# The first attention's last transposes ahead of the second pair's values, and part of the last tile's stores over three queues

## The chip, the cores and the metric

The kernel runs on one core of one Trainium2 chip. The metric is the device time of one launch in microseconds (us), as the median over several executions; a profile of one execution stands beside it.

## The reference

Sliding-window attention is followed by a feed-forward network. Batch 8, 8 heads, 576 positions, 64 elements per head; each query sees the keys at most 32 positions away. The feed-forward part takes 4608 tokens of 512 values through a hidden layer of 2048 with the tanh form of GELU. Everything is given and taken in float32.

```python
scores = (1 / sqrt(64)) * matmul(q, k.transpose(0, 1, 3, 2))      # q, k, v: (8, 8, 576, 64)
scores = where(abs(i - j) <= 32, scores, -1e9)
attn = softmax(scores)                                            # over the keys
x = matmul(attn, v).transpose(0, 2, 1, 3).reshape(4608, 512)
h = x @ w_in                                                      # 512 x 2048
g = 0.5 * h * (1 + tanh(c * (h + 0.044715 * h**3)))               # c = sqrt(2 / pi)
out = g @ w_out                                                   # 2048 x 512
```

## The kernel before

**Staging.** The attention works by batch `b` and by groups `g`: groups 0 to 3 are the four pairs of heads, group 4 is the tail of the positions. Its result goes, transposed, into a ring `xT`, from which the feed-forward part takes nine tiles `t` of 512 tokens. Batch `b = t + 1` is computed while tile `t` is in its second product (`ffn_out`), after a table (`PLAN`) that names at which matmul which piece is emitted. There is no scheduler behind this: each engine executes its instructions in the order in which the program writes them, and waits only where data or a buffer is missing.

**The start.** Batch 0 has no tile to lie beside. All of its inputs, the weights and the inputs of batch 1 come over SP's queue, one DMA after the other, in the written order: q and k by pairs (`qk`), v by heads (`vs`), then the float32 weights in four blocks (`load_w_in`: the first in two halves, which bring rows 0 to 1 and 2 to 3 of the block's four), batch 1's q and k, and w_out. GpSimd (POOL) casts most of it to float16: q and k by pairs (`cast_early`, L253), v by pairs (`cast_v`, L263), the first two weight blocks (`cast_w`, L190).

For a group the chain is: TensorE transposes q and k (`turn`, L282 and L284) into the PSUM bank `x0`; VectorE (DVE) copies them out (`trans_out`, L289 and L290); TensorE makes the scores (`score`, L354); ScalarE (ACT) takes the exponential (L360); VectorE multiplies with a mask (`mask`, L369); TensorE sums values and weights (`weighed`, L387; it needs the cast v of its pair); ScalarE inverts the sums as exp(-ln) (L401, L402); VectorE multiplies (`spread`, L411) into `xT`. `spin` issues matmuls of 512 columns on zeros that nothing reads.

After that come the first columns of the first product, `ffn_in(0, fc, d0, d1)` (L446): `d0` to `d1` is the part of the 512 rows of w_in taken, and pair `d` of `xT` is what it is multiplied with. Columns 0 to 3 take block 0 of w_in, columns 4 to 7 block 1.

**The end.** The last tile (t = 8) is combined from seven products of half the size (`ffn_out`, n counts them, and `ffn_last`). Its results leave as they become final: two quarter-tiles after n = 2 (on SP), two after n = 4, two after n = 5, two in `ffn_last`. A quarter-tile of 128 tokens is stored in two to five pieces, because batches and positions cut it; of n = 4 and n = 5 there are seven pieces each. Earlier tiles are stored by GpSimd's queue.

**Waits of the DMAs.** In the built program the DMAs of SP and ACT carry one of eight counters in turn, in one common sequence, and each waits, before it is issued, until the DMA that had the same counter eight places before has landed. GpSimd's DMAs have eight counters of their own.

Of the kernel before, what the change touches and what calls it, by code (L numbers as in the profile page):

```python
# [29 lines left out]
def cut(b):  # L30
    return 120 if b else 128


def width(pieces):
    return sum(4 * (p1 - p0) for (_, _, p0, p1) in pieces)
# [26 lines left out]
def kernel(  # L62
# [9 lines left out]
    nc = tc.nc  # L72
# [5 lines left out]
    NT = NTOK // 512  # L78
# [98 lines left out]
    def stage_w():  # L177
        return stage.tile([128, 4, 512], FP32, name="wst", tag="stage")

    def load_w_in(i, w, c0=0, c1=4):  # L180
        nc.sync.dma_start(w[:, c0:c1, :], w_in_v[:, c0:c1, 512 * i:512 * i + 512])  # L181
        return w
# [5 lines left out]
    def cast_w(w, dst, on_dve=2, cs=range(4)):  # L188
        for c in cs:
            (nc.vector if c < on_dve else nc.gpsimd).tensor_copy(dst[:, c, :], w[:, c, :])  # L190

    qk, tails, vs, vtail = load_early(0)
# [6 lines left out]
    qk(6)  # L199
    vs(2, 3)  # L200
    vs(4, 5)
    wi = [load_w_in(0, stage_w(), 0, 2)]
    vs(6, 7)
    load_w_in(0, wi[0], 2, 4)
    wi[1:] = [load_w_in(i, stage_w()) for i in range(1, 4)]

# [4 lines left out]
    def spin(n, width, score=False):  # L211
        ps = psS.tile([128, 2, 512], FP32, name="spin2", tag="S0")[:, 0, :] if score else \
            psO.tile([128, 512], FP32, name="spin", tag="O")
        for _ in range(n):
            nc.tensor.matmul(ps[:, 0:width], idle[:, 0:128], idle[:, 0:width], start=True, stop=True)
# [12 lines left out]
    for i in (0, 3, 4, 1, 2):  # L228
        m, off = masks[i], 0
# [30 lines left out]
    def cast_v(b, pr):  # L260
        vr = raws[b][3]
        hs = slice(2 * pr, 2 * pr + 2)
        nc.gpsimd.tensor_copy(Vs[b % 2][:, 0:4, hs, :], vr[:, :, hs, :])  # L263
# [24 lines left out]
    def trans_out(b, pr, pt):  # L288
        nc.vector.tensor_copy(QTs[b][:, pr, :, 0:128], pt[:, 0:4, :])  # L289
        nc.vector.tensor_copy(  # L290
            KTs[b % 2][:, pr, 0:512].rearrange("d (p j) -> d p j", j=4),
            pt[:, 4:8, :].rearrange("d j p -> d p j"))
# [37 lines left out]
    def halves_of(b, g):  # L330

        if g < 4:
            return [(masks[0], [g], MAIN[0]),
                    (masks[1], [g], MAIN[1]) if b else (masks[3], [g], MAIN_0[1])]
        return [(masks[2], range(NPAIR), TAIL) if b else (masks[4], range(NPAIR), TAIL_0)]
# [9 lines left out]
    def score(b, g):  # L345
        pes = []
        for hf, (m, prs, pieces) in enumerate(halves_of(b, g)):
            w = width(pieces) * len(prs)
            ps = psS.tile([128, 2, 512], FP32, name="ps_s", tag=f"S{hf}")
            for (pr, k0, c, p0, p1, off) in placed(prs, pieces):  # L350
                n = p1 - p0
                for h in range(2):
                    r0 = 64 * h
                    nc.tensor.matmul(  # L354
                        ps[:, h, off:off + 4 * n].rearrange("k (j p) -> k j p", j=4),
                        KTs[b % 2][r0:r0 + 64, pr, k0:k0 + 128],
                        QTs[b][r0:r0 + 64, pr, :, p0:p1], start=True, stop=True)
            pe = ap_.tile([128, 2, w], FP16, name="pe", tag=f"pe{hf}") if g < 4 else \
                tailp.tile([128, 2, w], FP16, name="pet")
            nc.scalar.activation(pe, ps[:, :, 0:w], AF.Exp, scale=SCALE)  # L360
            pes.append(pe)
        groups[(b, g)] = pes
# [42 lines left out]
    def spread(b, g, o, lt):  # L405
        n = size(b, g)
        if g < 4:
            pos, done = b * S % RING, 0
            while done < n:
                e = min(n - done, RING - pos)  # L410
                nc.vector.tensor_tensor(xT[:, g, pos:pos + e], o[:, done:done + e],  # L411
                                        lt[:, done:done + e], op=ALU.mult)
                done, pos = done + e, (pos + e) % RING
        else:
            pos = (b * S + 4 * cut(b)) % RING
            assert pos + n // NPAIR <= RING
            nc.vector.tensor_tensor(
                xT[:, :, pos:pos + n // NPAIR], o[:, 0:n].rearrange("d (r q) -> d r q", r=NPAIR),
                lt[:, 0:n].rearrange("d (r q) -> d r q", r=NPAIR), op=ALU.mult)
# [72 lines left out]
    out_v = out.rearrange("(b p j) f -> b j p f", b=B, j=4)  # L492
    pys = {}

    turn_about = [nc.sync, nc.scalar]

    def store(t, t4, yo, cols=slice(0, 512), eng=None):
        m = 0
        while m < 128:
            b, c = divmod(t * 512 + t4 * 128 + m, S)  # L500
            q0, n = (0, cut(b)) if c < 4 * cut(b) else (cut(b), 144 - cut(b))
            j, p = divmod(c - 4 * q0, n)
            e = min(n - p, 128 - m)
            if t == NT - 1 and eng is None:
                turn_about.reverse()
            (eng or turn_about[0] if t == NT - 1 else eng or nc.gpsimd).dma_start(  # L506
                out_v[b, j, q0 + p:q0 + p + e, cols], yo[m:m + e, cols])
            m += e

    later = []  # L510
# [14 lines left out]
    def ffn_out(t, i):  # L525

        n, blk, f = i // 16, i // 8 % 2, i % 8
        if t == 1 and i > 2 and i in wino["todo"]:
            combine(i)
        a, w, new = WINO[n]  # L530
        end = t == NT - 1
        if i % 16 == 0 and new:
            pys[n % 2] = bank((first(t) + n) % 2)
            if end and n == 4:
                pys["apart"] = psO.tile([128, 512], FP32, name="py2", tag="O")
        py = pys[n % 2].rearrange("p (b c) -> p b c", b=2)
        apart = end and blk and n in (4, 6)
        if a[0] == "A":
            r0, c0 = 8 * (int(a[2]) - 1) + f, 256 * (int(a[1]) - 1) + 128 * blk
            lhsT = gTs[t][:, r0, c0:c0 + 128]  # L540
        else:
            lhsT = wino[a][:, f, 128 * blk:128 * blk + 128]
        one = end and n in (4, 6)
        nc.tensor.matmul(pys["apart"][:, 0:256] if apart else py[:, blk, :], lhsT,  # L544
                         wino[w][:, f, :], start=(new and i % (8 if one else 16) == 0),
                         stop=(i % (8 if one else 16) == (7 if one else 15)),
                         skip_group_check=True)
        if i % 16 < 15:
            return
        yo, left, right = wino["yo"], slice(0, 256), slice(256, 512)  # L550
        C11, C12, C21, C22 = (yo[:, r:r + 2, c] for r in (0, 2) for c in (left, right))

        M1, U2, U3 = C21, C12, C22
        if n == 0:
            nc.vector.tensor_copy(M1, py)
        elif n == 1:
            nc.vector.tensor_tensor(U2, py, M1, op=ALU.add)
        elif n == 2:
            nc.vector.tensor_copy(C11, py)
            if end:  # L560
                for x in range(2):
                    store(t, x, yo[:, x, :], left, nc.sync)
        elif n == 3:
            nc.vector.tensor_tensor(U3, py, M1, op=ALU.add)
        elif n == 4:
            if not end:
                nc.vector.tensor_tensor(C22, py, U3, op=ALU.add)
            else:
                for x, part in enumerate((py[:, 0, :], pys["apart"][:, 0:256])):
                    nc.vector.tensor_tensor(C22[:, x, :], part, U3[:, x, :], op=ALU.add)  # L570
                    store(t, 2 + x, yo[:, 2 + x, :], right)
        elif n == 5:
            nc.vector.tensor_tensor(C21, py, M1, op=ALU.add)  # L573
            for x in range(2):
                store(t, 2 + x, yo[:, 2 + x, :], left if end else slice(0, 512))
# [23 lines left out]
    cast_early(0, 3, both)  # L599
    cast_v(0, 1)  # L600
    cast_v(0, 2)
    cast_w(wi[0], w_in16[:, :, 0:512], 0, (0, 1))
    cast_v(0, 3)
    cast_w(wi[0], w_in16[:, :, 0:512], 0, (2, 3))


    qk, tails, vs, vtail = load_early(1)
# [4 lines left out]
    def turn(g):  # L612
        pt = bank16(0)
        trans_pair(0, g, pt, now=False)
        return pt
# [8 lines left out]
    pt = turn(1)  # L624
# [7 lines left out]
    pt = turn(2)  # L632
# [2 lines left out]
    mask(0, 1, (1,))  # L635
    weighed(0)
    score(0, 2)
    spread(0, 0, *ods[0])
    spin(5, 512)
    weighed(1)  # L640
    pt = turn(3)
    trans_out(0, 3, pt)
    mask(0, 2)
    spin(3, 512, score=True)
    score(0, 3)
    spread(0, 1, *ods[1])
    weighed(2)
# [34 lines left out]
    for fc in range(6, NF):  # L682
        if fc in TURN_0:
# [3 lines left out]
            if pr < 2:  # L687
                pt = psS.tile([128, 2, 8, 128], FP16, name="pt", tag=f"S{pr}")
# [8 lines left out]
    for t in range(NT):  # L697
        b = t + 1
# [18 lines left out]
        for i in range(113 if t else 65):  # L717
            for act in plan.get(i, "").split():
# [11 lines left out]
                elif kind == "t":  # L730
                    pt = psS.tile([128, 2, 8, 128], FP16, name="pt", tag="S1")
# [19 lines left out]
            if t == 0 and i in (38, 40, 55):  # L751
                t4, yo = later.pop(0)
# [41 lines left out]
```

The softmax here doesn't subtract the row's maximum and nothing guards it: scores larger than these inputs give would overflow.

## Time and profile before

| | us |
|---|---|
| median of 4 executions | 311.67 (310.79 to 313.68) |
| the profiled execution's own time | 311.07 |
| its span, first to last instruction | 309.3 |
| TensorE busy | 297.9 (96%) |
| ACT / DVE / POOL busy | 199.9 / 198.4 / 102.2 |
| mean granted TensorE clock | 0.999 |

Busy time of TensorE is modelled for the ends of the matmuls, which are pipelined; a matmul of 512 columns has 379 ns in the rows, while eight in a row take 1.73 us. "PEld" are its weight loads, "SPq", "ACTq" and "POOLq" the queues that issue DMAs. The moved bytes are 50.64 MB, of which 37.50 MB go over SP's queue.

### The profile page before, as it was taken

How to read it: one execution, taken by the hardware profiler on the slowest of the kernel's cores; microseconds unless marked ns; L12 is line 12 of the kernel's file. 1: busy time of each engine (PE TensorE's matmuls, PEld its weight loads, DVE VectorE, ACT ScalarE, POOL GpSimd, SP SyncE). 2: the span in 40 equal slices, each digit the busy share in tenths (PEclk: the TensorE clock that was granted, in tenths of full speed). 3: DMA queues.
4: the chain of work that ended last, by engine and by line, in shares of the span. 5: the costliest groups of instructions: out<-in, count | busy, mean ns of one | idle time of the engine just before them, and what ended most of it. 6: DMA issues, size and time to landing. Idle time of an engine off the chain costs nothing.

```text
span 309.3 us, 6731 instructions
## 1 busy us (share of the span) xinstructions
PE 297.9 (96%) x2643; PEld 187.1 (60%) x2643; DVE 198.4 (64%) x453; ACT 199.9 (65%) x315; POOL 102.2 (33%) x158
## 2 busy tenths in 40 slices
PE   6889999999999999999999999999999999999993
PEld 2553545445784588448854785478647864784583
DVE  5764587867968476947784678666866643632451
ACT  1776477477677776778676876677768676706600
POOL 2647455192029110921093108510710061006000
PEclk9999999999999999999999999999999999999999
DMA  7999999999998998899769965999391022004013
GB/s 200 255 343 370 374 343 199 311 162 149 176 220 192 158 215 119 149 161 230 144 171 155 254 105 140 155 217 172 92 168 34 2 71 67 2 0 136 2 37 100
DMA packets 120061, 50.64 MB, mean 164 GB/s; under 512 B 101327, under 2 KB 113359, under 8 KB 120030
## 3 DMA queue, kind: packets, MB, share of 16 engines
q1 hardware_dynamic: 84329, 37.50, 58.7%
q0 software_dynamic: 34768, 11.54, 30.7%
q10 hardware_dynamic: 933, 1.18, 1.2%
q8 instruction: 20, 0.33, 0.5%
q14 instruction: 11, 0.09, 0.1%
HBM read 37.62 MB, written 9.44 MB: 152 GB/s over the span
## 4 chain that ended last, share of the span: by engine, by line
PE 72%; SPq 12%; DMA 11%; DVE 3%; issue 1%; POOL 0%; DVEq 0%
PE mm L544 30%; PE mm L446 20%; PE ph L446 12%; SPq L139 5%; PE ps_o L387 4%; DMA wst<-in_moe_w_in_dram 3%; PE ps_s L354 3%; DMA qr<-in_q_dram 3%; PE ps_d L387 3%; DMA KT<-k 3%; DMA kr<-in_k_dram 2%; SPq L162 2%; SPq L130 2%; SPq L185 1%; SPq L181 1%
## 5 line engine op out<-in xcount | busy, mean ns | idle before, releaser
L446 PEld LDWEIGHTS <-w_in 128*128 128x128 f16 x576 | 56.0, 98 | 66.5 <-POOL w_in L190 1.3
L446 PE MATMUL mm<-xT,w_in 128*128 128x512 f16 x352 | 86.3, 379 | 0.5 <-DVE xT L411 0.5
L506 POOL DMA_DIRECT2D out_dram<-y x77 | 45.2, 594 | 115.5 <-DVE y L573 114.7
L454 ACT ACTIVATE gT<-mm 128x512 f16<-128x512 f32 x88 | 52.4, 599 | 37.1 <-PE mm L446 37.1
L446 PE MATMUL ph<-xT,w_in 128*128 128x512 f16 x224 | 58.7, 379 | 0.3 <-POOL w_in L190 0.3
L490 DVE TENSOR_TENSOR s<-gT 128x512 f16<-128x512 f16 x64 | 26.9, 420 | 42.1 <-ACT gT L454 42.1
L544 PEld LDWEIGHTS <-s 128*128 128x128 f16 x512 | 48.6, 98 | 7.5
L360 ACT ACTIVATE pe<-ps_s 128x704 f16<-128x704 f32 x64 | 43.3, 727 | 9.2 <-PE ps_s L354 9.2
L544 PE MATMUL mm<-t,s 128*128 128x256 f16 x376 | 45.7, 273 | 0.0
L401 ACT ACTIVATE lt<-ps_d 128x480 f32<-128x480 f32 (+3 forms) x40 | 22.2, 556 | 30.8 <-PE ps_d L387 30.8
L454 ACT ACTIVATE gT<-ph 128x512 f16<-128x512 f32 x56 | 33.0, 600 | 13.0 <-PE ph L446 12.9
L544 PEld LDWEIGHTS <-gT 128*128 128x128 f16 x384 | 36.0, 98 | 7.3
L544 PE MATMUL mm<-w_out,gT 128*128 128x256 f16 x256 | 32.8, 273 | 0.0
L369 DVE TENSOR_TENSOR pe<-pe,mask 128x704 f16<-128x704 f16 x64 | 31.2, 523 | 1.7 <-ACT pe L360 1.6
L411 DVE TENSOR_TENSOR xT<-ps_o,lt 128x480 f16<-128x480 f32 (+5 forms) x38 | 20.2, 549 | 12.5 <-ACT lt L402 12.5
L387 PEld LDWEIGHTS <-V 128*64 128x64 f16 x336 | 18.1, 109 | 10.7 <-issue 5.0
L402 ACT ACTIVATE lt<-lt 128x480 f32<-128x480 f32 (+3 forms) x40 | 23.5, 587 | 1.3
L387 PE MATMUL ps_o<-pe,V 128*64 128x160 f16 (+2 forms) x244 | 21.8, 241 | 0.8 <-POOL V L263 0.4
L87 ACT ACT_TABLE_LOAD x17 | 21.8, 1283 | 1.1 <-PEq L778 0.8
L387 PE MATMUL ps_d<-pe,ones 128*64 128x192 f16 (+2 forms) x264 | 22.4, 235 | 0.0
L170 POOL DMA_DIRECT2D V<-in_v_dram x24 | 22.0, 941 | 0.0
L354 PE MATMUL ps_s<-QT,KT 64*128 64x192 f16 (+5 forms) x336 | 17.9, 227 | 1.1 <-DVE KT L290 1.0
(77 smaller groups left out, 295.9 us busy)
## 6 DMA issues: line engine op xcount, KB each, us to landing
kr<-in_k_dram SPq DMA_DIRECT2D x32, 256.0 KB, 6.8
qr<-in_q_dram SPq DMA_DIRECT2D x6, 1024.0 KB, 7.7
V<-in_v_dram POOLq DMA_DIRECT2D x30, 128.0 KB, 7.9
wst<-in_moe_w_in_dram SPq DMA_DIRECT2D x3, 1024.0 KB, 8.3
wst<-in_moe_w_out_dram SPq DMA_DIRECT2D x3, 1024.0 KB
qr<-in_q_dram SPq DMA_DIRECT2D x8, 256.0 KB
vr<-in_v_dram SPq DMA_DIRECT2D x16, 128.0 KB, 7.5
out_dram<-y POOLq DMA_DIRECT2D x24, 48.0 KB, 2.3
```

Of the source, the lines that this page charges most:

```text
L170: nc.gpsimd.dma_start(V[:, c, :, :], v[b, :, 128 * c:128 * c + 128, :].rearrange("h p d -> p h d"))
L354: nc.tensor.matmul(ps[:, h, off:off + 4 * n].rearrange("k (j p) -> k j p", j=4), KTs[b % 2][r0:r0 + 64, pr, k0:k0 + 128], QTs[b][r0:r0 + 6 ...
L360: nc.scalar.activation(pe, ps[:, :, 0:w], AF.Exp, scale=SCALE)
L369: nc.vector.tensor_tensor(pe, pe, m.rearrange("p (o w) -> p o w", o=1).broadcast_to(list(pe.shape)), op=ALU.mult)
L387: nc.tensor.matmul(bk[r0:r0 + 64, at:at + 4 * n].rearrange("d (j p) -> d j p", j=4)[:, :, p0 - q0:p1 - q0], V[:, c, 2 * pr + h, :] if w == ...
L401: nc.scalar.activation(lt[:, 0:n], d[:, 0:n], AF.Ln)
L402: nc.scalar.activation(lt[:, 0:n], lt[:, 0:n], AF.Exp, scale=-1.0)
L446: nc.tensor.matmul(ph, w_in16[:, dc, fc * 128:fc * 128 + 128], xT[:, dc, t * 512 % RING:t * 512 % RING + 512], start=(dc == 0), stop=(dc = ...
L454: nc.scalar.activation(gTs[t][:, fc, :], phs[fc], AF.Gelu_apprx_tanh)
L490: nc.vector.tensor_tensor(dst, x, y, op=op)
L506: (eng or turn_about[0] if t == NT - 1 else eng or nc.gpsimd).dma_start(out_v[b, j, q0 + p:q0 + p + e, cols], yo[m:m + e, cols])
L544: nc.tensor.matmul(pys["apart"][:, 0:256] if apart else py[:, blk, :], lhsT, wino[w][:, f, :], start=(new and i % (8 if one else 16) == 0) ...
```

## The change

In the start, the v of heads 6 and 7 is loaded ahead of the first half of w_in's first block, where it was between the two halves; GpSimd's casts follow in the same order. In batch 0, `turn(3)` and `trans_out(0, 3)` stand directly after `score(0, 2)`, ahead of the weighing of pair 1; the spins there, five and three, become four in one place. In the end, the stores after n = 4 go round SP, GpSimd and ACT (GpSimd first) where they went round ACT and SP; those after n = 5 go round ACT and SP as before, but begin with ACT where they began with SP.

```diff
     vs(2, 3)
     vs(4, 5)
+    vs(6, 7)
     wi = [load_w_in(0, stage_w(), 0, 2)]
-    vs(6, 7)
     load_w_in(0, wi[0], 2, 4)
...
-    turn_about = [nc.sync, nc.scalar]
+    turn_about, three = [nc.sync, nc.scalar], [nc.sync, nc.gpsimd, nc.scalar]
...
             if t == NT - 1 and eng is None:
-                turn_about.reverse()
-            (eng or turn_about[0] if t == NT - 1 else eng or nc.gpsimd).dma_start(
-                out_v[b, j, q0 + p:q0 + p + e, cols], yo[m:m + e, cols])
+                turn_about.append(turn_about.pop(0))
+            if eng is three:
+                three.append(three.pop(0))
+            q_ = three[0] if eng is three else eng or (turn_about[0] if t == NT - 1 else nc.gpsimd)
+            q_.dma_start(out_v[b, j, q0 + p:q0 + p + e, cols], yo[m:m + e, cols])
...
                     nc.vector.tensor_tensor(C22[:, x, :], part, U3[:, x, :], op=ALU.add)
-                    store(t, 2 + x, yo[:, 2 + x, :], right)
+                    store(t, 2 + x, yo[:, 2 + x, :], right, three)
...
     cast_v(0, 2)
+    cast_v(0, 3)
     cast_w(wi[0], w_in16[:, :, 0:512], 0, (0, 1))
-    cast_v(0, 3)
     cast_w(wi[0], w_in16[:, :, 0:512], 0, (2, 3))
...
     score(0, 2)
+    pt = turn(3)
     spread(0, 0, *ods[0])
-    spin(5, 512)
+    trans_out(0, 3, pt)
+    spin(4, 512)
     weighed(1)
-    pt = turn(3)
-    trans_out(0, 3, pt)
     mask(0, 2)
-    spin(3, 512, score=True)
     score(0, 3)
```

## Prediction

> **What bounds the kernel now.** I read the page's slices first, then the chain of work that ended last, then the timeline around the two places of the change. The chain, in order of time, in three pieces:
>
> ```profile
> 14.61 0.52 SPq L181
> ...
> 15.69 10.50 DMA wst<-in_moe_w_in_dram
> ...
> 26.20 7.93 DMA qr<-in_q_dram
> ...
> 66.90 7.91 DMA KT<-k
> ...
> 74.86 0.46 PE ps_s L354 x8
> ```
>
> Up to 74.8 us the end is set by SP's stream of loads (weights, batch 1, batch 2, the transposes by DMA), not by the attention of batch 0. After that the chain is TensorE's matmuls nearly to the end. The slices agree: DMA is at 9 from the second slice on, at 340 to 374 GB/s while the weights come. Where the attention of batch 0 (12 to 24 us) meets that stream shows in the timeline (start, length, engine, what, idle before and who ended it):
>
> ```profile
> 17.30 1.17 POOL L190 CAST w_in<-wst 128x512 f16<-128x512 f32 x2 [0.87 <-DMA wst<-in_moe_w_in_dram]
> ...
> 19.47 0.61 POOL L263 CAST V<-vr 128x512 f16<-128x512 f32 x1 [1.00 <-DMA vr<-in_v_dram]
> ...
> 20.76 1.20 POOL L190 CAST w_in<-wst 128x512 f16<-128x512 f32 x2 [0.68 <-DMA wst<-in_moe_w_in_dram]
> ...
> 23.52 2.29 POOL L190 CAST w_in<-wst 128x512 f16<-128x512 f32 x4 [1.57 <-DMA wst<-in_moe_w_in_dram]
> ...
> 24.75 0.39 PE L446 MATMUL ph<-xT,w_in 128*128 128x512 f16 x1 [0.17 <-POOL w_in L190]
> ...
> 25.31 1.04 PE L446 MATMUL ph<-xT,w_in 128*128 128x512 f16 x4 [0.17 <-POOL w_in L190]
> ```
>
> To be seen: four loads end GpSimd's idle time one after another, and the last, block 1 of w_in at 23.52, is cast slice by slice while TensorE waits for each slice, the last time at 25.31. Whatever TensorE does before, it passes 25.31 no sooner unless that block lands sooner. Behind it there is next to no slack in the other direction: TensorE is busy 4.69 of the 4.70 us after 25.30, and it reached the scores at 74.86 about when the last transpose landed (busy 4.89 of the 5.00 us from 70). So an early gain is lost, and a delay beyond 25.31 is mostly paid.
>
> **The change part by part: the start.** *Loads.* Same DMAs, same bytes, same counter by place in the sequence; two of 128 KB (v of heads 6 and 7) go past one of 512 KB. What follows, block 0's second half included, keeps its place, so it should land as before: 20.76 and 23.52. Between lie, by the rows above, 19.47 - 17.30 = 2.17 us for the two v, 20.76 - 19.47 = 1.29 us for a half block. Reversed: v at 17.30 - 1.3 or so + 2.17, about 18.0 (was 19.47), and the first half at 19.47 (was 17.30). GpSimd's casts then run: v 18.0 to 18.6, first half 19.47 to 20.7 (two of 0.61), second half from 20.76 as before. GpSimd's queue loses nothing, since the second half is not there earlier.
>
> *Order of the attention.* ACT and DVE keep their sequences; on TensorE eight transposes go past the weighing of pair 1, and 8 spins become 4 (4 x 0.216 us less, with 1.73 us for eight). After `score(0, 2)` (13.62, 0.49 us) the transposes of q can start at once (q's cast ended at 13.55), those of k wait for the cast that ends at 14.51; TensorE is through at about 15.0, was 17.08. Queued behind this 0.4 us wait are four spins and the weighing of pair 1, which needed v's cast, at 15.62, anyway: it goes at 15.9 to 16.7, was 15.67 to 16.5, a loss of 0.2. DVE copies out after `spread(0, 0)` (ends 15.39, unmoved): 15.4 to 16.4, was 17.11 to 18.13. The wait removed is this one:
>
> ```profile
> 18.19 0.49 PE L354 MATMUL ps_s<-QT,KT 64*128 64x160 f16 x10 [0.47 <-DVE KT L290]
> ```
>
> `score(0, 3)` goes at 16.7 (was 18.19), mask 2 at 16.4 to 17.65 (18.05 to 19.31), weighing of pair 2 at 17.25 to 18.1 (18.89 to 19.9). The gain shrinks at once on ACT, which has, in order, ln and exp of pair 1 (0.60 + 0.63), two exponentials of pair 3 (1.46), ln and exp of pair 2 (1.23): from 16.8 they end at 20.7, were 21.2. So `spread(0, 2)` ends at 21.4, was 21.94. What is late next is TensorE's following instruction, `ffn_in(0, 0)`: it needs the first half's casts, at 20.1 and 20.7, ran at 19.84 before; behind it in the queue stands the weighing of pair 3, so at 20.95 to 21.85 (was 20.51 to 21.45), 0.4 later. Then six matmuls to 23.15, four to 24.0, and column 4, whose weights are there at 24.19 as before. `spread(0, 3)` comes at about 23.25 to 23.95 (was 22.86), wanted only after 26. **Sum of the start: 0.0 us.** The cover is the arrival of block 1; it leaves 0.2 us at 24.19 and some 0.6 at 25.31. If block 0 landed half a microsecond later than I say, that would still be hidden. Bounds for the start: a loss of 0.7 (both halves landing together at 20.76: casts to 23.2, column 5 done at 26.8 instead of 26.18); a gain of 0.5, if the denser order let block 1 land that much earlier (nothing in the rows says so).
>
> **TensorE's idle time** [...]. Between the weighing of pair 2 (18.1) and `ffn_in(0, 0)` (20.1) it now stands for about 2.0 us with no spin, where the largest gap of that stretch was about half a microsecond. The trace has one long pause, at the end: the last matmul ends at 304.5, and the granted clock (third value from the end of each row; before it the busy time of TensorE, weight loads, DVE, ACT and POOL, after it DMA share and GB/s) is
>
> ```profile
> 307.50:308.00 0.50, 0.00 (x0) 0.00 (x0) 0.00 (x0) 0.00 (x0) 0.00 (x0) 1.00 0.00 0
> 308.00:308.50 0.50, 0.00 (x0) 0.00 (x0) 0.00 (x0) 0.00 (x0) 0.00 (x0) 0.93 0.00 0
> 308.50:309.30 0.80, 0.00 (x0) 0.00 (x0) 0.00 (x0) 0.00 (x0) 0.00 (x0) 0.50 0.04 10
> ```
>
> so full for some 3.8 us of idling, then half. [...] I take the row: 0.0. If the cover were gone, see the third rival.
>
> **The end.** These are the last DVE result and the last issues, and the waits that SP makes in the store line:
>
> ```profile
> 304.56 0.42 DVE L582 TENSOR_TENSOR y<-py,y 128x256 f32<-128x256 f32 x1 [0.45 <-PE py L544]
> ...
> 305.01 0.80 ACTq L506 DMA_DIRECT2D out_dram<-y  x2
> ...
> 305.59 0.74 SPq L506 DMA_DIRECT2D out_dram<-y  x2
> ...
> L506 SPq EVENT_SEMAPHORE  x4: 17/17/17, 300.0 to 305.5; - x4
> ```
>
> SP's last two stores hold what DVE finished at 304.10, yet go out at 305.59: the first has the counter of an 88 KB store that ACT issued at 303.53, and a wait on SP ends at 305.5. That gives 1.96 us from issue to release. The last issue ends at 306.33, and the span 3.0 us later.
>
> With the change, three of the seven pieces after n = 4 (40, 24 and 24 rows) go to GpSimd, and the counters of all later stores shift. GpSimd: start at 300.65 when DVE is done, 594 ns each by its 77 rows, the second and third after DVE's 301.48, so done by 302.7; 2.3 us to landing (its 48 KB stores; nearest row, for the smaller 16 KB ones it is 2.5): 305.2 at most, two microseconds before the last store lands. Cost 0.0; nobody waits for its counters. After n = 5 ACT issues four pieces from 303.53 (to 305.01, as SP's four did), SP three (to 304.74). Last pieces: SP's 56 rows have a long-landed counter and go at 304.8; SP's 72 rows have that of the 88 rows which SP now issues at 303.53, so 305.5 + 0.09 to 305.95. ACT's 48 rows have that of 40 rows issued at 303.53: 305.5, not 305.01, to 305.87; its 80 rows that of 32 rows issued at 303.87: 303.87 + 1.96 = 305.83, to about 306.27. **Sum: 306.27 against 306.33, -0.05 us**: the wait moves from SP to ACT. Bounds: -0.5 (no counter waited for: ACT's last issue ends at 305.81) and +0.3 (the 40 and 32 rows landing as late as 2.3 us).
>
> [...]
>
> **Total.** 311.07 of the profiled execution - 0.05 = 311.0. The profiled execution is 0.6 below the median of the runs shown, so the same kernel measured anew is 311.67 - 0.05 = **311.6**.
>
> **Rivals.**
> 1. *No change*, as summed: 311.6. Chance 0.72.
> 2. *The end gains its bound*, because landings are quicker than 1.96 us for small pieces: 311.67 - 0.5 = 311.2. For it: two of ACT's four waits hang on pieces of 40 and 32 rows. Against: 80 rows still go last behind another store. 0.10.
> 3. *Slower by the clock.* If the first half of w_in came so late [...], it would work at half clock from there: 12 matmuls (2.6 us) and a weighing (0.9) double, +3.5, of which 0.6 is slack and about 1.2 is taken by later waits of TensorE (0.25 at 31.46, 0.36 at 37.88, 0.19 at 39.73, 0.38 at 46.80). About +1.7: 313.4; without those waits +2.9, 314.6. For it: the spins have gone just there. Against: the same half lands 1.3 us ahead of a load that keeps its place. 0.08.
> 4. *The attention is on the path after all*: the 0.5 us by which `spread(0, 2)` comes earlier, or all of the 1.5 of `score(0, 3)`, reaches the end: 311.2 to 310.2. Against: the wait at 25.31. 0.06.
> The rest, 0.04, is a start that the loads' new order stretches or shortens by a microsecond or more.
>
> **Numbers.** The runs before spread by 2.9 us, so the median itself is good to about 1 us; with the bounds (-1.0 and +1.0 together) and part of rival 3 the range is 309.9 to 313.3. About 1%, 3.1 us, is what a measurement of this kernel can tell from no change: faster 0.02, within 0.93, slower 0.05, the last mostly rival 3.
>
> **What would show it.** Right: GpSimd's w_in casts again from 20.76 and 23.52, L446 waiting for them to 25.3, the L290 wait before `score(0, 3)` gone, a TensorE gap of 2 us before 20.1 at full clock, the KT transposes landing at 74.8, and an ACT wait at 305.8 ahead of the last store. Wrong: block 1 cast before 23.2 or after 23.8, a clock below 1.00 between 18 and 26, a last issue before 305.9 or after 306.6, or GpSimd's stores landing last.

## The result, and the profile after

Median 312.54 us (311.06 to 314.54, 44 executions) against 311.69 us for the kernel before (310.46 to 313.73, 63 executions): a ratio of 1.0027, 95% interval 1.0017 to 1.0038. The change costs **0.85 us** (0.5 to 1.2). That is within 1%, and within the range of the prediction, but it is a loss that many executions resolve, where the forecast was 0.05 us of gain. The profiled execution took 312.19 us, with a span of 310.2.

From the page, the span and the granted clock in 40 slices of 7.8 us:

```profile
span 310.2 us, 6725 instructions
...
PEclk9989999999999999999999999999999999999998
```

The third digit is new: the clock of TensorE falls in the third slice (15.5 to 23.3 us), just where the change thinned its work. The timeline of the start of the changed kernel (start, length, engine, what, idle before and who ended it):

```profile
18.15 0.61 POOL L263 CAST V<-vr 128x512 f16<-128x512 f32 x1 [1.30 <-DMA vr<-in_v_dram]
19.41 2.61 POOL L190 CAST w_in<-wst 128x512 f16<-128x512 f32 x4 [0.65 <-DMA wst<-in_moe_w_in_dram]
...
20.08 0.39 PE L446 MATMUL mm<-xT,w_in 128*128 128x512 f16 x1 [1.69 <-POOL w_in L190]
...
20.96 0.39 PE L446 MATMUL mm<-xT,w_in 128*128 128x512 f16 x1 [0.49 <-POOL w_in L190]
...
23.46 2.29 POOL L190 CAST w_in<-wst 128x512 f16<-128x512 f32 x4 [1.44 <-DMA wst<-in_moe_w_in_dram]
...
27.14 0.59 PE L446 MATMUL mm<-xT,w_in 128*128 128x512 f16 x2
```

In it the casts of v, of the first half and of block 1 of w_in stand where the prediction put them (18.0, 19.47, 23.52), and so do the first two matmuls of `ffn_in(0, 0)` (20.1 and 20.7). But the last row is late. It is the matmul pair that begins the last column of block 1, and in the kernel before it stands here:

```profile
26.18 0.59 PE L446 MATMUL mm<-xT,w_in 128*128 128x512 f16 x2
```

From the first cast of block 1 that is 26.18 - 23.52 = 2.66 us before and 27.14 - 23.46 = 3.68 us after. The table of stretches shows what lies between (us; then busy time and count of TensorE, weight loads, VectorE, ScalarE, GpSimd; then granted clock, DMA share, GB/s). The changed kernel:

```profile
18.00:20.00 2.00, 0.40 (x14) 0.30 (x8) 1.56 (x3) 2.00 (x4) 1.20 (x3) 1.00 1.05 388
20.00:21.40 1.40, 0.82 (x6) 0.31 (x8) 1.08 (x2) 0.69 (x2) 1.40 (x3) 0.99 1.03 395
21.40:24.80 3.40, 3.40 (x26) 1.98 (x25) 0.74 (x2) 2.01 (x3) 1.96 (x5) 0.50 1.05 393
```

The kernel before, same stretches:

```profile
18.00:20.00 2.00, 1.60 (x31) 1.33 (x32) 2.00 (x5) 1.44 (x3) 1.00 (x2) 1.00 1.02 335
20.00:21.40 1.40, 1.34 (x22) 0.88 (x20) 1.07 (x3) 1.19 (x3) 0.72 (x3) 1.00 1.02 392
21.40:24.80 3.40, 2.75 (x19) 1.14 (x13) 1.24 (x2) 2.51 (x3) 1.83 (x4) 1.00 1.05 393
```

TensorE pauses between 18.4 and 21.0, twice (1.69 and 0.49 us); its clock is full all through the pauses and is halved afterwards, from 21.38 to 24.79 by the clock's own records, 3.41 us in which TensorE had work at every moment. Counted from the first cast of block 1, batch 1's first transposes begin 8.55 us later, where the kernel before takes 7.94 us: of the 1.02 us, 0.61 us are left there.

What becomes of them further on, these two profiles do not show. Tile 1 begins its first product at 60.73 (60.12 before) and tile 2 at 93.00 (92.57 before). But two kernels of the experiments below, the end alone and ACT first, have the start of the kernel before and a full clock in it, and their tile 2 begins at 93.00 and 93.09. And the chain of work that ended last in the changed kernel does not pass the late matmuls. At that time it runs through SP's loads:

```profile
15.79 10.32 DMA wst<-in_moe_w_in_dram
...
26.14 7.97 DMA qr<-in_q_dram
```

From the start of tile 2 to that of tile 8 every one of the thirteen profiled executions takes 185.74 us. So what tells them apart lies ahead of tile 2, or behind the last VectorE result.

The second part of the loss is at the end. The last VectorE row and the stores of the last tile, after:

```profile
304.99 0.42 DVE L584 TENSOR_TENSOR y<-py,y 128x256 f32<-128x256 f32 x1 [0.45 <-PE py L546]
...
L509 ACTq DMA_DIRECT2D out_dram<-y x8: 306/348/560, 301.1 to 306.5; - x8
L509 ACTq EVENT_SEMAPHORE  x4: 17/17/17, 292.8 to 305.9; - x4
```

The rows of one line give min, median and max length in ns, then first and last start. Last result to end of the span is 310.2 - 305.41 = 4.79 us; before it was 309.3 - 304.98 = 4.31 us (unrounded spans). I call this the **closing time**. So the 0.9 us between the two spans are 0.43 us from ahead of the end, which is no more than two executions of one kernel can differ by, and 0.48 us of closing time, which repeats from profile to profile (next section).

### The profile page after: what moved, and what is told of

Its sections match the earlier page's. It is cut to its first block, busy times and chain, and to the rows that moved or that the text cites. A ratio compares the mean times of both kernels' runs of the same rounds, so it can differ in the third digit from the quotient of the medians.

```text
span 310.2 us, 6725 instructions
## 1 busy us (share of the span) xinstructions
PE 297.7 (96%) x2639; PEld 187.9 (61%) x2639; DVE 198.9 (64%) x453; ACT 199.7 (64%) x315; POOL 103.7 (33%) x161
## 4 chain that ended last, share of the span: by engine, by line
PE 71%; SPq 11%; DMA 11%; DVE 4%; issue 1%; POOL 0%; DVEq 0%
PE mm L546 30%; PE mm L446 19%; PE ph L446 12%; SPq L139 5%; PE ps_o L387 4%; DMA wst<-in_moe_w_in_dram 3%; PE ps_s L354 3%; DMA KT<-k 3%; DMA qr<-in_q_dram 3%; PE ps_d L387 2%; DMA kr<-in_k_dram 2%; SPq L162 2%; SPq L130 2%; SPq L185 1%; DVE k L318 1%
## 5 line engine op out<-in xcount | busy, mean ns | idle before, releaser
L509 POOL DMA_DIRECT2D out_dram<-y x80 | 46.7, 591 | 133.2 <-DVE y L575 114.7
L387 PEld LDWEIGHTS <-ones 128*64 128x64 f16 x336 | 18.8, 111 | 0.2 <-issue 0.2
```

Of the source, the lines that this page charges most:

```text
L387: nc.tensor.matmul(bk[r0:r0 + 64, at:at + 4 * n].rearrange("d (j p) -> d j p", j=4)[:, :, p0 - q0:p1 - q0], V[:, c, 2 * pr + h, :] if w == ...
L509: q_.dma_start(out_v[b, j, q0 + p:q0 + p + e, cols], yo[m:m + e, cols])
```

## The experiments

Eleven kernels were run. Two of their numbers are used: the ratio to the kernel before on the same chip, and, from the one profiled execution of each, the closing time and the half-clock stretch of the start.

| kernel | ratio (95%) | closing time, us | half clock in the profiled start, us | executions with mean clock under 0.996 |
|---|---|---|---|---|
| before | 1 | 4.31 | none | 1 of 129 |
| after | 1.0027 (1.0017 to 1.0038) | 4.79 | 21.38, for 3.41 | 35 of 44 |
| start alone | 1.0007 (0.9988 to 1.0026) | 4.32 | none | 9 of 14 |
| end alone | 1.0013 (0.9991 to 1.0035) | 4.72 | none | 2 of 14 |
| after, with six spins | 1.0013 (0.9996 to 1.0030) | 4.76 | none | 1 of 22 |
| loads alone | 0.9996 (0.9976 to 1.0016) | 4.29 | none | 0 of 14 |
| attention order alone | 0.9999 (0.9983 to 1.0015) | 4.31 | 21.44, for 3.41 | 7 of 14 |
| start, with six spins | 1.0015 (0.9993 to 1.0036) | 4.29 | none | 1 of 14 |
| start, no spins | 1.0014 (0.9996 to 1.0032) | 4.33 | 21.96, for 3.41 | 12 of 14 |
| before, no spins | 0.9992 (0.9977 to 1.0007) | 4.28 | 15.94, for 6.83 | 14 of 14 |
| ACT first | 0.9996 (0.9977 to 1.0015) | 4.46 | none | 0 of 12 |
| n = 5 on three queues | 1.0057 (1.0038 to 1.0077) | 6.08 | none | |
| tile 0's stores moved | 1.0148 (1.0115 to 1.0182) | 4.46 | 21.87, for 3.41 | 4 of 4 |

A mean clock under 0.996 is the sign of a half-clock stretch inside the run: the profiled executions that have one in the start lie at 0.989 to 0.995, the others with the old end at 0.998 to 1.000. The clock also falls after the last matmul (at 308.10 in the profile of the changed kernel), and in kernels with a longer end this blurs the sign (the end alone: 0.995 in its profiled execution, with no such stretch in the start; the kernel with n = 5 on three queues is left out for it).

**The start alone**: the kernel before with the new order of loads, casts and attention.

```diff
+    vs(6, 7)
     wi = [load_w_in(0, stage_w(), 0, 2)]
-    vs(6, 7)
...
+    cast_v(0, 3)
     cast_w(wi[0], w_in16[:, :, 0:512], 0, (0, 1))
-    cast_v(0, 3)
...
+    pt = turn(3)
     spread(0, 0, *ods[0])
-    spin(5, 512)
+    trans_out(0, 3, pt)
+    spin(4, 512)
     weighed(1)
-    pt = turn(3)
-    trans_out(0, 3, pt)
     mask(0, 2)
-    spin(3, 512, score=True)
```

> The start of the change alone (loads, order of batch 0's attention, spins); the stores of the last tile stay as before. Theory A (half clock): the TensorE pause of about 1.7 us ahead of ffn_in(0, 0) brings the granted clock to 0.5 for some 3 us from about 21.3 us on; TensorE leaves the start about 1 us late and 0.4 to 0.6 us of that reach the end: ratio 1.0013 to 1.002, granted mean clock about 0.99, last DVE result near 305.4 (was 304.98). Rival B (all in the stores): ratio 1.000, although the clock falls. Rival C (the reordered loads disturb the stream of DMAs): slower, whatever the clock, with block 1's cast or the K transposes of batch 2 later.

Measured: 312.11 us, ratio 1.0007. The profiled execution shows nothing: full clock, and the last column's matmuls at 25.69, which is 2.66 us behind the first cast of block 1 (23.03), as in the kernel before. Its stretches of time:

```profile
18.00:20.00 2.00, 0.33 (x1) 0.10 (x1) 1.82 (x3) 1.97 (x4) 1.34 (x3) 1.00 1.02 368
...
21.40:24.80 3.40, 3.19 (x24) 1.31 (x18) 0.69 (x1) 2.51 (x3) 1.98 (x5) 1.00 1.05 393
```

The same pause, and no loss of clock. Theory A's ratio (1.0013 to 1.002) was not met either. But of its 14 executions nine have a mean clock under 0.996, with a mean time of 312.33 us, and five do not, with 311.66. So the pause costs the clock in some executions of one and the same program and not in others, and one profile of it proves neither. That the nine are also the slower ones need not be the clock's doing: an execution whose loads land late has a longer pause and a longer time both.

**The end alone**: the changed kernel with the start undone (the diff above backwards).

> The end of the change alone (three queues after n = 4, ACT first after n = 5); the start as before. Theory A (the whole loss is the half clock): ratio 1.000, clock 1.00. Rival B (the stores): ratio 1.0013 or more, the time from the last DVE result to the end of the span 4.7 to 4.8 us instead of 4.3. Both together, as the two profiles suggest: about 1.001 here and about 1.0015 for the start.

Measured: 312.21 us, ratio 1.0013; closing time 4.72. The interval of the ratio takes in no change, but the closing time does not scatter: 4.28 to 4.33 in the seven profiled executions with the old end (before, and six of the kernels in the table), 4.72 to 4.79 in the three with the new one. The end costs 0.4 to 0.5 us, and not a gain of 0.05.

**The changed kernel with six spins** in TensorE's pause:

```diff
     weighed(2)
+    spin(6, 512, score=True)
     mask(0, 3)
```

> The whole change with six more spins in the pause after the weighing of pair 2 (into the bank S0, so from about 18.9 us, for 1.3 us). Theory A: the clock stays at 1.00 from 18 to 26 us, TensorE reaches the first dc = 3 matmul at 26.2 us as before instead of 27.1, and the ratio falls by 0.0015 to 0.002 below the 1.0027 of the whole change: 1.0005 to 1.001, what is left being the stores. If the clock has no part in it: 1.0027 again, or more, since six matmuls of 0.216 us were added.

Measured: 311.78 us, ratio 1.0013; a low clock in one execution of 22, against 35 of 44 without the spins. The stretch in question of its profile, to compare with 0.40 of the changed kernel:

```profile
18.00:20.00 2.00, 1.69 (x7) 0.53 (x6) 1.24 (x3) 1.72 (x3) 0.96 (x2) 1.00 1.01 366
```

So it is TensorE's idling there that costs the clock. What the clock costs in time is not resolved by this run: 1.0013 is 0.4 us less than 1.0027 and somewhat more than the 1.0005 to 1.001 expected, but the two intervals overlap. The closing time, 4.76, is that of the changed kernel.

**The loads alone, and the attention order alone**, the two halves of the start's diff.

> The order of loads and casts alone: v of heads 6 and 7 ahead of the first half of w_in's block 0; the attention's order and its eight spins stay. Theory A: the weighing of pair 2 still ends at about 19.9 us, so that the pause before ffn_in(0, 0) is at most 0.3 us, clock 1.00, ratio 1.000. Rival C (the stream of DMAs): the loss of the start stays here, ratio 1.001 or more.

> The order of batch 0's attention alone (transposes of pair 3 ahead of the weighing of pair 1, four spins for eight); loads and casts stay as before. So ffn_in(0, 0) finds its weights at 18.5 us and runs at about 19.0, and the wait moves to the weighing of pair 3, whose v is cast at 20.1: two pauses of 0.6 and 1 us instead of one of 1.7. Theory A (clock): fewer executions below 0.996 than the 9 of 14 of the whole start, and the median in between, ratio 1.000 to 1.001. If the loads' order is what costs, 1.000 without any below 0.996.

Measured: 311.60 us, ratio 0.9996, never a low clock for the loads; 312.08 us, ratio 0.9999, seven of 14 with low clock (mean 312.31 against 311.67 for the other seven) for the order. The order of the attention, which takes spins away and leaves pauses, brings the loss of clock, though none of time that the ratio shows; the order of the loads alone does not. The profiled executions of both are no measure of the start itself: with the loads alone block 1 came at 24.41 and tile 2 at 94.3, in an execution of 312.79 us that lies 1.2 us above the kernel's own median.

**The start with six spins**, to have the start alone without its loss of clock.

> The start of the change alone, with six more spins in the pause after the weighing of pair 2. Theory A (half clock for one stretch of 3.41 us[...]): no execution with a mean clock below 0.996, ratio 1.000, so that the start by itself neither gains nor loses. If the reordering costs by something else than the clock: 1.001 or more.

Measured: 312.69 us, ratio 1.0015 (0.9993 to 1.0036), a low clock in one of 14. This does not fit: without the loss of clock, and with the old end, nothing should be lost. The interval takes in both no loss and 1.1 us. In its profile block 1 comes late (first cast at 24.18), but from there to batch 1's first transposes it is 7.94 us, as in the kernel before. It is the one run that speaks for a cost of the start beside the clock, and it is not settled.

**The start without its four spins**, to lengthen the pause:

```diff
     trans_out(0, 3, pt)
-    spin(4, 512)
     weighed(1)
```

> The start of the change alone, without the four spins that it keeps: TensorE is idle for 0.9 us more, some 3 us ahead of the pause. Theory A: more executions with a mean clock below 0.996 than with the four spins (there 9 of 14), nearly all, and the median 0.5 to 0.8 us above before: ratio 1.0015 to 1.0025. If the clock costs nothing: ratio as without the loss, 1.000, whatever the clock.

Measured: 312.34 us, ratio 1.0014, just under the 1.0015 to 1.0025 expected, with an interval that takes in no loss; 12 of 14 with low clock, mean 312.41 against 311.67 for the other two. In its stretches TensorE does nothing at all for two microseconds, and the clock is full then and low later:

```profile
18.00:20.00 2.00, 0.00 (x0) 0.00 (x0) 1.44 (x3) 1.97 (x4) 1.10 (x2) 1.00 0.91 346
...
21.40:24.80 3.40, 3.40 (x24) 1.51 (x19) 0.69 (x1) 2.51 (x3) 1.90 (x4) 0.58 1.04 392
```

**The kernel before without its spins**, to ask whether half clock always costs:

```diff
     spread(0, 0, *ods[0])
-    spin(5, 512)
     weighed(1)
...
     mask(0, 2)
-    spin(3, 512, score=True)
     score(0, 3)
```

> The kernel before with nothing changed but the eight spins of the weighing of pair 1 and of score(0, 3) left out: data, loads and waits as before, TensorE idle for about 1.6 us before 15.7 and 1.1 us before 18.2. Theory A: the clock falls in part of the executions (mean below 0.996) and those are 0.3 to 0.6 us slower than the others; with most of them falling, ratio 1.001 to 1.0015. If the half clock is hidden by the loads: 1.000, however many fall.

Measured: 311.46 us, ratio 0.9992: no loss, though all 14 executions have a low clock, and the profiled one has twice the half-clock time of the changed kernel:

```profile
16.00:18.00 2.00, 1.88 (x24) 1.58 (x20) 0.08 (x1) 1.14 (x3) 0.53 (x1) 0.50 1.14 305
18.00:20.00 2.00, 1.00 (x16) 0.84 (x18) 2.00 (x4) 0.69 (x2) 1.47 (x3) 0.50 1.00 360
20.00:21.40 1.40, 1.40 (x21) 1.23 (x18) 1.40 (x3) 1.00 (x3) 1.40 (x3) 0.50 1.05 396
21.40:24.80 3.40, 3.31 (x29) 1.76 (x28) 2.09 (x4) 2.58 (x5) 2.24 (x5) 0.80 1.04 388
```

It is over at 22.77 (the 0.80 of the last row), before block 1's first cast at 23.44. One would think that its delay is hidden behind the arrival of that block. It is not; the last column's matmuls begin 3.42 us behind the cast, against 2.66 in the kernel before:

```profile
26.86 0.59 PE L446 MATMUL mm<-xT,w_in 128*128 128x512 f16 x2
```

Batch 1's first transposes begin 8.28 us behind the cast. All eight profiled executions with a full clock in the start have 7.92 to 7.94 us there. Of those with half clock the changed kernel, the start without spins and the kernel with tile 0's stores moved have 8.47 to 8.55, but the attention order alone has 7.94, although its half clock lies across the arrival of block 1. So the plain form of the theory, "a half-clock stretch costs", is not borne out by this run, and the place of the stretch does not sort the kernels either. Behind the transposes the profiles no longer tell a half clock from a full one: from there to tile 1 it is 28.5 to 30.0 us with either. Leaving out the spins also takes 1.73 us of work from TensorE, which could offset part of a loss.

**ACT first**, the new order of the stores after n = 5, with nothing on GpSimd:

```diff
             nc.vector.tensor_tensor(C21, py, M1, op=ALU.add)
+            if end:
+                turn_about.reverse()
             for x in range(2):
```

> The kernel before with one edit: the stores after n = 5 begin with ACT, as in the change; GpSimd stores nothing there. In the built program the last four stores then wait for the same pieces as in the change (48 rows on ACT for the 40 rows, 80 on ACT for the 32, 72 on SP for the 88). Theory W (the end loses by these waits): from the last DVE result to the end of the span 4.6 to 4.8 us, as with the whole change (4.79), against 4.32 before. Theory G (the end loses by GpSimd's stores or its drain of 5.57 us): 4.3 us.

Measured: 311.74 us, ratio 0.9996; closing time 4.46. That is between the two theories. Beginning with ACT moves the wait and puts 80 rows last, as in the changed kernel, and costs 0.15 us of closing time; the other 0.3 came with the stores after n = 4 (by the last run below, through the counters that they turn).

**The stores after n = 5 on three queues**, GpSimd's share in the place where SP and ACT are short of time:

```diff
...
             for x in range(2):
-                store(t, 2 + x, yo[:, 2 + x, :], left if end else slice(0, 512))
+                store(t, 2 + x, yo[:, 2 + x, :], left if end else slice(0, 512),
+                      three if end else None)
```

> The kernel before with three of the seven pieces after n = 5 (40, 24 and 24 rows) on GpSimd instead of pieces after n = 4. The last four stores then wait for pieces of n = 4 alone, which have long landed. Theory W: the last issue ends at DVE's last result + 0.83 us (before: + 1.34), last DVE result to end of span 3.8 to 4.0 us. Theory G, by the drain on GpSimd's queue, which in the changed kernel ended 5.0 us after its last store was issued: it would end at about 310.1 and the span 0.8 us later, 5.9 us after DVE's last result.

Measured: 313.63 us, ratio 1.0057 (+1.8 us), closing time 6.08, near theory G's 5.9. The last issue did end early, 0.83 us after the last VectorE result against 1.34 before, as theory W had it, but the span did not. What ended the span is in the rows of the program's closing line (L792 here):

```profile
L792 SPq EVENT_SEMAPHORE  x11: 17/28/2034, 306.3 to 312.3; - x11
...
L792 POOLq DRAIN  x3: 46/102/5641, 305.9 to 312.0; - x3
```

SP waits 2.03 us for the landing of GpSimd's last store; with that it is through its list at 309.7. But GpSimd's own closing instruction, DRAIN, lasts from 305.89 to 311.53, and only then do all engines meet.

**Tile 0's stores moved** to GpSimd in the changed kernel. Three stores fewer on ACT turn the common sequence of the eight counters by three places more, as the change itself had turned it by three, and alter nothing else at the end:

```diff
-                store(0, t4, yo, eng=nc.scalar)
+                store(0, t4, yo, eng=nc.gpsimd)
```

> The whole change, and tile 0's three stores of ACT moved to GpSimd, which takes three more places out of the common sequence of counters of SP and ACT. The stores of the end are the same in queue, order and what they wait for; but the last to land (80 rows on ACT) now has the last but one counter in SP's closing list of waits, where it had the second. Theory L (part of the end's loss is the list, some 65 ns for each wait that stands behind the last landing): last DVE result to end of span 4.4 to 4.5 us instead of 4.79. Without it: 4.75 to 4.8. The total time is not told apart by so little; the profile's end is what counts here.

Measured: closing time 4.46, as theory L had it, with the stores, queues and waits of the changed kernel, which has 4.79. The total is 315.99 us, ratio 1.0148, for a reason far from the end: VectorE waits at tile 0 until one of the moved stores has landed and its buffer is free,

```profile
63.86 0.69 DVE L521 COPY yo<-mm 128x512 f32<-128x512 f32 x1 [2.63 <-DMA out_dram<-yo]
```

and tile 2 starts at 95.14 (93.0 in the changed kernel). So this kernel tests the closing time, not the total.

## Why the prediction was wrong

**Right, and of no help.** The timeline of the start held: v at 18.15 (said 18.0), the first half at 19.41 (19.47), `ffn_in(0, 0)` at 20.08 and 20.96 (20.1 and 20.7), block 1 unmoved at 23.46 (23.52), a pause of TensorE ahead of 20.1. At the end the wait moved to ACT as said, with GpSimd's stores landed before anybody asked for them. The first transpose of KT landed at 74.84 by its counter (said 74.8). Two of the signs of being wrong came true: the clock was below 1.00 between 18 and 26, and the last issue ended at 306.80, after 306.6.

**Wrong first: "I take the row: 0.0" for TensorE's idle time.** The row was one sample, the clock going down 3.8 us behind the last matmul of one execution. In the profiled execution of the end alone it went down 2.2 us behind it (304.96 to 307.17), and in others up to 5 us (the changed kernel with six spins). So the row did not say how long an idling is free. The clock's records show more. In four executions the half clock starts at 21.38, 21.44, 21.87 and 21.96, when TensorE is at work again. Each of these stretches lasts 3.41 us, the long one of the kernel before without spins 6.83, twice as much, and the time at full clock in the two main profiles is a whole number of them too: in the changed kernel 17.07 us is five and 283.31 is 83, in the kernel before 303.79 is 89. In the 3.41 us ahead of the fall TensorE was busy for 1.2 us in the changed kernel, with no pause of two microseconds, for 1.7 us in the attention order alone, whose pauses are all under 0.8 us, and for 1.64 and 1.65 us in the start without spins and in the kernel with tile 0's stores moved. The first two of these stretches, in this order, each from its own kernel's table:

```profile
17.97:21.38 3.41, 1.23 (x19) 0.62 (x16) 2.62 (x4) 2.72 (x5) 2.58 (x4) 1.00 1.04 393
```

```profile
18.03:21.44 3.41, 1.72 (x31) 1.03 (x28) 2.54 (x4) 2.73 (x5) 2.86 (x4) 1.00 0.90 294
```

Laid end to end from the clock's first record in the profiles before and after, 177 such stretches have full clock. The clock fell behind three of them, in which TensorE was busy for 1.23 and 0.26 us (after) and 0.00 us (before, behind its last matmul), and behind none of the others, which have 1.82 us or more, in the profile's modelled busy time. From these rows, as an estimate: the sum of work in such a stretch counted here, not the longest pause. The profiled execution of the start alone fits it. Its clock fell at 308.89 only, and counted back from there by 3.41 us the pause is shared between two stretches:

```profile
15.34:18.75 3.41, 2.48 (x51) 2.11 (x50) 2.97 (x6) 2.71 (x5) 1.27 (x3) 1.00 1.04 291
18.75:22.17 3.42, 2.01 (x25) 1.23 (x26) 1.79 (x3) 1.85 (x4) 2.61 (x4) 1.00 1.04 387
```

But in the same profile TensorE is busy for only 1.24 us (0.33 + 0.91) from 18.00 to 21.40, with no fall behind it, so the place of the stretch must count too, and what sets that place was not shown. One and the same program has the low clock in some executions and not in others: 35 of 44 here, 9 of 14 for the start alone.

The third rival had a lower clock at this place, but only for a much later first half of w_in, and so got 0.08 of the chance; it also doubled 3.5 us of work, where the measured 3.41 us at half clock delay work by half of that, 1.7 us, at most (an estimate). What the lower clock costs in time is an estimate: low-clock executions against the others of the same kernel are 0.24 us apart in the changed kernel, 0.67 in the start alone, 0.64 in the attention order alone and 0.74 without spins. Weighted by their numbers, at a scatter of 0.78 us of a single execution, that is 0.47 us, give or take 0.4. Times 35/44 it makes some 0.4 us of the 0.85. It is not a cost that was shown, since late loads would lengthen the pause and the time both, and since the time did not clearly follow where an edit alone changed the clock: six spins took the changed kernel from 1.0027 to 1.0013, but the start from 1.0007 to 1.0015, and the kernel before without its spins, at low clock in all executions, lies at 0.9992.

**Wrong second, and the larger part: the end sum, -0.05.** Measured, the closing time grew by 0.48 us. The sum itself was off by little: the last issue ended 1.39 us behind the last VectorE result, where it has 1.29 and the kernel before 1.34. But it stopped at the end of the last issue, and took what comes after it, "the span 3.0 us later", as fixed. The records of the closing instructions show what that time consists of. SP waits for the eight counters in a fixed order, some 60 to 90 ns for each, with one stall of 0.40 to 0.42 us somewhere in it; then all engines meet. The terms, from the last VectorE result (us):

| | before | ACT first | after | tile 0's stores moved |
|---|---|---|---|---|
| last store issued | 0.97 | 1.02 | 1.06 | 1.04 |
| its landing seen by SP | 2.83 | 3.01 | 3.03 | 2.99 |
| place of its counter among the eight | fifth | fifth | second | seventh |
| from there to the end | 1.48 | 1.45 | 1.76 | 1.47 |
| closing time | 4.31 | 4.46 | 4.79 | 4.46 |

The last store of the changed kernel, 80 rows, is seen 0.20 us later than the 72 rows that were last before: its issue is 0.09 later, the rest is its landing. This the kernel with ACT first repeats. And the store's counter is the second of the list, so that six waits are still to be made behind it; turned by three places, it is the seventh and 0.29 us are back. Together 0.2 + 0.3 = 0.48 us. The bound of +0.3 that I gave for the end was therefore too small, because the list had no term in it.

**GpSimd's part of the end** was right in its cost of 0.0, with less room than I thought. Its closing DRAIN in the changed kernel:

```profile
L790 POOLq DRAIN  x3: 46/93/5567, 302.6 to 309.9; - x3
```

It ends at 308.19, and the engines meet at 309.46: 1.3 us to spare, not the two microseconds of the stores' landing. The kernel with n = 5 on three queues shows the same wait in the open.

**What stays open.** The end's 0.48 us are shown. The other 0.4 us, give or take as much, are not: the estimate for the clock is of that size, but its interval reaches nearly to zero. The nine executions of the changed kernel with full clock lie 0.66 us (give or take 0.6) above the mean of the kernel before, which is as near to the closing time alone as to the whole loss, and the start with six spins lay at 1.0015. Whether the clock costs these tenths, or the new order of the start without it, the runs do not settle: a single execution scatters by 0.78 us, and block 1 came anywhere between 23.03 and 24.41 in the profiled executions, the orders mixed.

## What to carry to other kernels

Spins that look like waste may keep the clock for work that comes two microseconds later (a low clock in 35 of 44 executions of the changed kernel, in one of 22 with six spins more): before taking them away, add up TensorE's busy time around the pause, and do not look at the longest pause alone (in the start the clock fell behind 1.23 to 1.72 us of work in 3.41 us), and ask what has no slack in the stretch after it. A clock that falls is not yet a loss of time; follow the delay to the chain that ends last. At the end of a kernel, count to the end of the span: the landing of the last store, the place of its counter in the closing waits, and what each queue that has been used still has to close. A lone sample in a trace (one fall of the clock) bounds nothing; a quantity that repeats to 0.07 us in ten profiles, as the closing time did, settles what 14 timed executions leave open.

## What was not expected of the hardware

The clock was full during the pauses and half during the work behind them, for 3.41 us to the hundredth (6.83 in one case); in the attention order alone three pauses of under 0.8 us each (0.74, 0.46 and 0.49) stood ahead of the fall. Behind the last matmul it fell after 2.2 to 5 us, according to the execution.

GpSimd's closing DRAIN ended 4.97 to 4.98 us after the end of its last DMA issue in all five kernels that store there late (303.21 to 308.19 in the changed kernel, 306.56 to 311.53 with n = 5 on three queues, 305.36 to 310.33 with tile 0's stores moved), though its last store had landed 1.8 us after that issue in the second of them. From there to the end of the span it was another 0.8 us in that kernel (311.53 to 312.32). By these two times, an estimate: a store that GpSimd issues in the last 5.8 us or so of a kernel like this one holds up the end, whatever it relieves.
